# State read of both halves of the heads at once: eight transposes into two banks, 64 records into one

## The chip, the cores and the metric

One core of one Trainium2 chip runs the whole program. The metric is device time in microseconds (us); lower is better. A quoted time is the median of several executions; a profile is one execution of its own.

## What is computed

Attention between tokens and a small state, both ways, and then a feed-forward layer over all rows. Cut to what matters:

```python
B, H, S, Ns, D = 8, 8, 512, 32, 64          # x: (B,H,S,D), state: (B,H,Ns,D), fp32
a  = softmax(x @ state.T / sqrt(D));  xread = a @ state      # 512 rows per batch
a2 = softmax(state @ x.T / sqrt(D));  sread = a2 @ x         # 32 rows per batch: the state read
y  = concat([xread, sread], axis=2) as (B*544, 512)          # d_model 512
h  = y @ w_in;  g = h - tanh(h);  out = g @ w_out            # d_ff 2048
```

## The kernel before

The 4096 token rows go through the feed-forward layer as eight chunks of 512 rows, one per batch, and the 256 state rows as a ninth. A chunk is 16 steps. A step's `hidden(f)` makes one 128-row slice of h in a bank of the pool `ps_h` (two banks) by six matmuls of 512 columns (L461 to L463), then tanh on ScalarE (ACT) and subtractions on VectorE (DVE) make g. `output(f)`, two steps later, adds twelve matmuls (L508 to L510) into four output banks. These matmuls, and those of lines L922 in the second half of the run, are called the main matmuls here; their names are hps, ops, X and Y.

Chunks 0 to 3 run in this way. Chunks 4 to 7 are taken two at a time by `Pair`, whose products (L922, X and Y) take weights back from DRAM (W0m, W1m) and where DVE adds and subtracts whole pieces of g (names G, g0m, g1m). Chunk 8 is the state rows.

Beside the main matmuls stands side work. It is cut into units by `yield`, and a table gives the step at which each unit is written (`ASIDE`, keyed att1 to att7, a0, r1, m0; `SIDES` for the pairs). A scheduler then orders each engine's instructions, with `issue_after` and `high_priority` as its bounds. Each engine runs its list in order, so a matmul that waits holds all that stand behind it. Side work that matters here:

- `attention(b)`: loads xT of both halves of the heads, scores (`all_scores`, names sps, 16 short records into two banks), softmax on DVE and ACT.
- `state_read(b)` (names s, pps, p2t, rps, sr): for each half hf in turn, a softmax of s (`reduce_max` on DVE, Exp on ACT, 1/sum on DVE), a load of xn, four 128x128 transposes of s into one bank (pps), one copy to p2t on ACT, a yield, then 16 matmuls (32 records in a profile) of 32 weight columns and 64 moving columns into a second bank (rps), which are held together by `issue_after` and `high_priority`, and four scaled copies into `sr` on ACT, another yield. Batches 0 and 1 run it late, under the table's keys a0 and r1.
- `m_units` (m0 in the table): products mps and mls, copied by ACT to `st` and `sl` and stored to DRAM by 8 DMAs of the SP queue per unit (md<-st, md<-sl).

`free` is every copy out of the pool `ps_a` (two banks); each is issued after the one before. `behind_free(made)` makes a matmul wait for the last such copy, so that two banks are taken together. pps, rps, sps and mps all live in `ps_a`. The tiles of xT and xn share two buffers (tag "x"), so the loads of the next batch's xT wait until the matmuls on xn are through. All DMAs of this part are issued by SP, in order.

Of the kernel before, what the change touches and what calls it, by code (L numbers as in the profile page):

```python
# [19 lines left out]
P = 128  # L20
# [15 lines left out]
def attention_ffn(ctx: ExitStack, tc: tile.TileContext, xT, xn, bd, bh, sp, sm, sl, win, wout, xout, tout, sout):  # L36
# [10 lines left out]
    nc = tc.nc  # L47
# [6 lines left out]
    ps_a = ctx.enter_context(tc.tile_pool(name="ps_a", bufs=2, space=PSUM))  # L54
# [14 lines left out]
    ident = cpool.tile([P, P], F32, name="ident")  # L69
# [15 lines left out]
    def bank(p, name):  # L85
        return p.tile([P, 512], F32, tag=p.name, name=name)
# [105 lines left out]
    def free(out, src, **more):  # L192

        with ExitStack() as behind:
            if freed[0] is not None:
                behind.enter_context(tc.issue_after(freed[0]))
            made = nc.scalar.activation(out, src, AF.Copy, **more) if more else nc.scalar.copy(out, src)
        freed[0] = made.ins

    def behind_free(made):  # L200
        if freed[0] is not None:
            info = mybir.DependencyInfo(mybir.DependencyClass.Sync, mybir.DependencyReason.DATA)
            tc.add_manual_dep(made.ins, freed[0].name, info, reason="both banks free")
# [85 lines left out]
    def attention(b, aT):  # L289
# [76 lines left out]
        if b >= EARLY_S:  # L366
            yield from state_read(b, ss)
        else:
            late[b] = ss
# [4 lines left out]
    def late_read(b):  # L374
        yield from state_read(b, late[b])
# [3 lines left out]
            split(aTs[0][:, 0, hf], aTs[0][:, 1, hf], ats[hf])  # L379

    def state_read(b, ss):
        for hf in range(2):

            s = ss[hf]
            m2 = pool.tile([P, 1], F32, tag="m2", name=f"m2{b}{hf}")
            nc.vector.reduce_max(m2, s, axis=AX.X)
            nm = pool.tile([P, 1], F32, tag="nm", name=f"nm{b}{hf}")
            nc.vector.tensor_scalar_mul(nm, m2, -SCALE)
            rs = pool.tile([P, 1], F32, tag="rs", name=f"rs{b}{hf}")
            nc.scalar.activation(s, s, AF.Exp, bias=nm, scale=SCALE, accum_out=rs)  # L390
            ri = pool.tile([P, 1], F32, tag="ri", name=f"ri{b}{hf}")
            nc.vector.tensor_scalar_add(ri, rs, EPS)
            nc.vector.reciprocal(ri, ri)
            xr = pool.tile([P, 4, 256], F32, tag="x", name=f"xn{b}{hf}", bufs=XB)
            with tc.issue_after(loadlog[min(len(loadlog) - 1, XH)]):
                nc.sync.dma_start(xr, xn[b, hf])
            ps = bank(ps_a, f"pps{b}{hf}").rearrange("p (k n) -> p k n", n=P)
            for k in range(4):
                nc.tensor.transpose(ps[:, k], s[:, k * P : (k + 1) * P], ident)
            pt = pool.tile([P, 4, P], F32, tag="p2t", name=f"p2t{b}{hf}", bufs=PTB)  # L400
            free(pt, ps)
            yield

            ps = bank(ps_a, f"rps{b}{hf}")[:, :64]
            run = []
            for k in range(4):
                for c in range(4):
                    cs = slice(32 * c, 32 * c + 32)
                    j = TURN[c] if b < 2 else c
                    with ExitStack() as behind:  # L410
                        if run:
                            behind.enter_context(tc.issue_after(run[-1]))
                            behind.enter_context(tc.high_priority())
                        made = nc.tensor.matmul(  # L414
                            ps[cs], pt[:, k, cs], xr[:, k, 64 * j : 64 * j + 64], start=(k == 0), stop=(k == 3)
                        )
                    run.append(made.ins)
            for j in range(4):
                h = 4 * hf + (TURN[j] if b < 2 else j)
                js = slice(32 * j, 32 * j + 32)  # L420
                free(
                    sr[b // 4][32 * (b % 4) : 32 * (b % 4) + 32, 64 * h : 64 * h + 64],
                    ps[js],
                    scale=ri[js],
                )
            yield

    def turn_sread():
        srT = pool.tile([P, 2, 4, 256], F32R, tag="aT", name="srT", bufs=AB)
# [154 lines left out]
    xrs = [pool.tile([P, 2, 512], F32, tag="x", name=f"xT0{hf}", bufs=XB) for hf in range(2)]  # L584
# [12 lines left out]
    wb, mps, sps_ps, hps, ss = {}, {}, {}, {}, {}  # L597
# [99 lines left out]
    FILL = json.loads('[1, 0, 1, 2]')  # L697
    afters = [firstDVE[0], tanhs[0][1], tanhs[1][1]]
    a0 = state_read(0, ss)
    split_first()  # L700
    late1 = late_read(1)
# [3 lines left out]
    for p in range(2):  # L705
# [13 lines left out]
        a0=[1, 1, 3, 3],  # L719
# [14 lines left out]
    if "att0" in SCH:  # L734
# [4 lines left out]
        "att1": D0["att"]["1"],  # L739
        "att2": [16 + x for x in (3, 4, 5, 6, 6, 8, 8, 9, 9)],  # L740
        "m0": [17, 18, 19, 20, 22, 23, 24, 25, 26, 27, 28, 29, 30, 31, 33, 34],
        "att3": [30, 31, 31, 32, 33, 35, 36, 37, 38],
        "a0": [38, 40, 42, 44],
        "att5": [39, 40, 41, 42, 43, 45, 46, 48, 49],
        "att4": [46, 47, 48, 49, 50, 53, 55, 57, 59],
        "att6": [62, 62, 62, 63],
        "r1": [52, 54, 56, 58],
    }
    AHEAD = [54, 56, 58, 60, 62, 63]
    KEEP = [20 + x for x in range(16)]  # L750
# [222 lines left out]
    for n, duo in enumerate(duos):  # L973
        a, b = duo.a.i, duo.b.i
# [112 lines left out]
```

## Time and profile before

| what | us |
|---|---|
| median of 3 runs | 673.16 (672.67 to 675.13) |
| the profiled execution | 671.88 |
| its span, first to last instruction | 670.1 |
| TensorE matmuls busy in it | 640.1 (96%) |
| TensorE weight loads busy | 494.6 (74%) |
| VectorE busy | 485.0 (72%) |
| ScalarE busy | 391.3 (58%) |

The rows below come from views of that one execution. A timeline row gives the start and the length of one instruction or of a run of equal ones (xN), and in brackets how long the engine had been idle and whose end released it. Since matmuls overlap, a busy time says little of TensorE's pace: the distance from one start to the next does.

### The profile page before, as it was taken

The page shows a single profiled execution, that of the slowest core. Times are in us where ns is not written, and L with a number is a line of the kernel's source. Part 1 is how long each engine was busy: PE and PEld are TensorE (multiplying, and loading weights), DVE is VectorE, ACT ScalarE, POOL GpSimd, SP SyncE. Part 2 cuts the span into 40 slices and gives each one's busy share as a digit, 9 for nine tenths or more (in the row PEclk, how much of TensorE's full clock was granted, in tenths as well). Part 3 has the DMA queues.
Part 4 walks back from the last instruction along what each step waited for, and adds up shares of the span by engine and source line. Part 5 has one row for each costly group of instructions (what it writes and reads, how often), then busy time and mean ns, then how long its engine had stood idle before and what let it go on. Part 6 is the DMA issues. An engine that isn't in the chain of part 4 may idle for free.

```text
span 670.1 us, 9663 instructions
## 1 busy us (share of the span) xinstructions
PE 640.1 (96%) x3482; PEld 494.6 (74%) x3482; DVE 485.0 (72%) x769; ACT 391.3 (58%) x675; POOL 26.9 (4%) x41
## 2 busy tenths in 40 slices
PE   6778989999999999999999999999999999999997
PEld 3446666677766677787787777778888888788996
DVE  5999998639545597989735958896965689754442
ACT  3768874658655576675745667445665654543532
POOL 2000000000000000000000000000000000333300
PEclk9899998999999999999999999999999999999999
DMA  9798897466758876646722444564565535899800
GB/s 310 212 346 320 279 373 246 138 181 188 214 169 260 252 228 210 217 140 209 249 97 100 138 147 144 200 204 142 157 189 169 177 126 158 285 327 334 283 28 31
DMA packets 65199, 137.01 MB, mean 204 GB/s; under 512 B 6784, under 2 KB 28544, under 8 KB 65152
## 3 DMA queue, kind: packets, MB, share of 16 engines
q1 hardware_dynamic: 62592, 128.02, 58.8%
q0 software_dynamic: 2560, 8.39, 3.7%
q8 instruction: 27, 0.44, 0.3%
q14 instruction: 20, 0.16, 0.1%
HBM read 93.91 MB, written 42.47 MB: 204 GB/s over the span
## 4 chain that ended last, share of the span: by engine, by line
PE 55%; DVE 8%; DMA 3%; ACT 2%; SPq 1%; issue 1%; ACTq 0%; DVEq 0%
PE X L922 11%; PE hps L461 7%; PE hps L463 6%; PE hps L462 6%; PE Y1m L922 5%; PE ops L508 4%; PE ops L510 4%; PE ops L509 4%; PE Y0m L922 4%; DMA md<-st 1%; DMA mr<-md 1%; DVE G L475 1%; DVE m L101 1%; PE rps L414 1%; SPq L247 1%
## 5 line engine op out<-in xcount | busy, mean ns | idle before, releaser
L509 PE MATMUL ops<-wo,g 128*128 128x512 f32 x256 | 100.9, 398 | 5.4 <-DVE wo L101 5.4
L461 PE MATMUL hps<-aT,m 128*128 128x512 f32 x248 | 100.0, 405 | 5.0 <-DVE G L475 2.0
L508 PE MATMUL ops<-wo,g 128*128 128x512 f32 x256 | 95.8, 403 | 1.3 <-ACT wo L101 0.8
L462 PE MATMUL hps<-aT,m 128*128 128x512 f32 x248 | 97.0, 391 | 0.0
L463 PE MATMUL hps<-aT,m 128*128 128x512 f32 x248 | 96.5, 391 | 0.0
L510 PE MATMUL ops<-wo,g 128*128 128x512 f32 x256 | 93.2, 399 | 0.1
L477 DVE TENSOR_TENSOR t<-hps,t 128x512 f32<-128x512 f32 (+1 forms) x78 | 49.0, 630 | 48.3 <-ACT t L477 47.9
L475 ACT ACTIVATE t<-hps 128x512 f32<-128x512 f32 x64 | 38.2, 598 | 53.9 <-PE hps L463 53.8
L477 ACT ACTIVATE t<-hps 128x512 f32<-128x512 f32 (+1 forms) x78 | 43.0, 554 | 45.0 <-PE hps L463 42.6
L475 DVE TENSOR_TENSOR G<-hps,t 128x512 f32<-128x512 f32 x64 | 43.7, 687 | 32.3 <-ACT t L475 32.3
L461 PEld LDWEIGHTS hps<-aT,m 128*128 128x128 f32 x248 | 46.5, 188 | 24.4 <-DVE G L475 4.5
L508 PEld LDWEIGHTS ops<-wo,g 128*128 128x128 f32 x256 | 48.3, 190 | 19.4 <-ACT wo L101 2.9
L509 PEld LDWEIGHTS ops<-wo,g 128*128 128x128 f32 x256 | 48.5, 190 | 18.1 <-DVE wo L101 7.6
L101 ACT CAST g<-t 128x512 fp32r<-128x512 f32 (+1 forms) x78 | 44.9, 578 | 25.3 <-DVE t L477 24.6
L101 DVE TENSOR_TENSOR g<-t,g 128x512 fp32r<-128x512 f32 (+1 forms) x78 | 48.8, 629 | 13.1 <-ACT g L101 12.7
L510 PEld LDWEIGHTS ops<-wo,g 128*128 128x128 f32 x256 | 48.6, 191 | 11.3 <-DVE g L101 0.5
L463 PEld LDWEIGHTS hps<-aT,m 128*128 128x128 f32 x248 | 46.6, 188 | 10.4 <-DVE m L101 0.4
L462 PEld LDWEIGHTS hps<-aT,m 128*128 128x128 f32 x248 | 46.8, 189 | 8.8
L922 PE MATMUL X<-g0m,W0m 128*128 128x512 f32 x192 | 47.2, 391 | 0.4 <-DVE g0m L101 0.4
L960 POOL DMA_DIRECT2D wl<-wod x32 | 23.3, 729 | 600.1 <-DVE g1m L101 563.9
L922 PE MATMUL X<-g1m,W1m 128*128 128x512 f32 x192 | 46.0, 391 | 0.6 <-DVE g1m L101 0.6
L101 ACT CAST g1m<-G 128x1024 fp32r<-128x1024 f32 x28 | 29.2, 1054 | 28.9 <-PE Y1m L922 12.7
(257 smaller groups left out, 1131.3 us busy)
## 6 DMA issues: line engine op xcount, KB each, us to landing
mr<-md SPq DMA_DIRECT2D x24, 512.0 KB, 3.9
xT<-in_xT SPq DMA_DIRECT2D x16, 512.0 KB, 4.9
wod<-wo SPq DMA_DIRECT2D x32, 256.0 KB, 5.7
md<-st SPq DMA_DIRECT2D x64, 128.0 KB, 2.4
xn<-in_xn SPq DMA_DIRECT2D x16, 512.0 KB, 5.0
wsd<-ws SPq DMA_DIRECT2D x16, 512.0 KB, 4.8
W0m<-wsd SPq DMA_DIRECT2D x16, 512.0 KB, 4.1
W1m<-wsd SPq DMA_DIRECT2D x16, 512.0 KB, 4.5
```

The source lines that it names most:

```text
L101: return nc.scalar.copy(hi, src), (sub or nc.vector).tensor_sub(lo, src, hi)
L247: nc.sync.dma_start(dst.rearrange("h n f -> n h f"), stage[32 * j : 32 * j + 32])
L461: nc.tensor.matmul(ps, mhi[k][:, cols], ahi[:, k], start=(k == 0), stop=False)
L462: nc.tensor.matmul(ps, mhi[k][:, cols], alo[:, k], start=False, stop=False)
L463: made = nc.tensor.matmul(ps, mlo[k][:, cols], ahi[:, k], start=False, stop=(k == nk - 1))
L475: main(nc.scalar.activation(t, ps, AF.Tanh), nc.vector.tensor_sub(g, ps, t))
L477: tanhs.append((nc.scalar.activation(t, ps, AF.Tanh).ins, nc.vector.tensor_sub(t, ps, t).ins))
L508: nc.tensor.matmul(o, g[:, 0, tok], w[:, 0], start=(f == 0), stop=False)
L509: nc.tensor.matmul(o, g[:, 0, tok], w[:, 1], start=False, stop=False)
L510: return nc.tensor.matmul(o, g[:, 1, tok], w[:, 0], start=False, stop=(f == NFF - 1)).ins
L922: made = nc.tensor.matmul(out[t], w[:, e, x, cols], y[:, e], start=first and j == 0 and e == 0 and c == 0, stop=last and j == 3 and e == 1 ...
L960: nc.gpsimd.dma_start(wo[f][:, :, cols].bitcast(F32), wod[:, f % 2, half, f // 2])
```

## The change

`state_read` first does the softmax of both halves (a yield after each), then both loads of xn, then all eight transposes in a row into two banks (half 1 first; the first of them waits by `behind_free` for the last copy out of `ps_a`), both copies to p2t, a yield, and then 32 matmuls (64 records) in a row into one bank, half 0 in columns 0 to 63 and half 1 in columns 64 to 127. Eight scaled copies follow. The number of yields stays at four. The table's steps of att3, a0, att5, att4 and r1 are rewritten. No instruction is added or taken away.

```diff
@@ -379,6 +379,7 @@
             split(aTs[0][:, 0, hf], aTs[0][:, 1, hf], ats[hf])
 
     def state_read(b, ss):
+        ris, xrs, pts = [], [], []
         for hf in range(2):
 
             s = ss[hf]
@@ -391,18 +392,34 @@
             ri = pool.tile([P, 1], F32, tag="ri", name=f"ri{b}{hf}")
             nc.vector.tensor_scalar_add(ri, rs, EPS)
             nc.vector.reciprocal(ri, ri)
+            ris.append(ri)
+            yield
+        for hf in range(2):
             xr = pool.tile([P, 4, 256], F32, tag="x", name=f"xn{b}{hf}", bufs=XB)
             with tc.issue_after(loadlog[min(len(loadlog) - 1, XH)]):
                 nc.sync.dma_start(xr, xn[b, hf])
-            ps = bank(ps_a, f"pps{b}{hf}").rearrange("p (k n) -> p k n", n=P)
+            xrs.append(xr)
+        pss = [bank(ps_a, f"pps{b}{hf}").rearrange("p (k n) -> p k n", n=P) for hf in range(2)]
+        run = []
+        for hf in (1, 0):
             for k in range(4):
-                nc.tensor.transpose(ps[:, k], s[:, k * P : (k + 1) * P], ident)
+                with ExitStack() as behind:
+                    if run:
+                        behind.enter_context(tc.issue_after(run[-1]))
+                        behind.enter_context(tc.high_priority())
+                    made = nc.tensor.transpose(pss[hf][:, k], ss[hf][:, k * P : (k + 1) * P], ident)
+                if not run:
+                    behind_free(made)
+                run.append(made.ins)
+        for hf in range(2):
             pt = pool.tile([P, 4, P], F32, tag="p2t", name=f"p2t{b}{hf}", bufs=PTB)
-            free(pt, ps)
-            yield
-
-            ps = bank(ps_a, f"rps{b}{hf}")[:, :64]
-            run = []
+            free(pt, pss[hf ^ 1])
+            pts.insert(0, pt)
+        yield
+
+        ps = bank(ps_a, f"rps{b}")
+        run = []
+        for hf in range(2):
             for k in range(4):
                 for c in range(4):
                     cs = slice(32 * c, 32 * c + 32)
@@ -412,18 +429,23 @@
                             behind.enter_context(tc.issue_after(run[-1]))
                             behind.enter_context(tc.high_priority())
                         made = nc.tensor.matmul(
-                            ps[cs], pt[:, k, cs], xr[:, k, 64 * j : 64 * j + 64], start=(k == 0), stop=(k == 3)
+                            ps[cs, 64 * hf : 64 * hf + 64],
+                            pts[hf][:, k, cs],
+                            xrs[hf][:, k, 64 * j : 64 * j + 64],
+                            start=(k == 0),
+                            stop=(k == 3),
                         )
                     run.append(made.ins)
+        for hf in range(2):
             for j in range(4):
                 h = 4 * hf + (TURN[j] if b < 2 else j)
                 js = slice(32 * j, 32 * j + 32)
                 free(
                     sr[b // 4][32 * (b % 4) : 32 * (b % 4) + 32, 64 * h : 64 * h + 64],
-                    ps[js],
-                    scale=ri[js],
+                    ps[js, 64 * hf : 64 * hf + 64],
+                    scale=ris[hf][js],
                 )
-            yield
+        yield
 
     def turn_sread():
         srT = pool.tile([P, 2, 4, 256], F32R, tag="aT", name="srT", bufs=AB)
@@ -739,12 +761,12 @@
         "att1": D0["att"]["1"],
         "att2": [16 + x for x in (3, 4, 5, 6, 6, 8, 8, 9, 9)],
         "m0": [17, 18, 19, 20, 22, 23, 24, 25, 26, 27, 28, 29, 30, 31, 33, 34],
-        "att3": [30, 31, 31, 32, 33, 35, 36, 37, 38],
-        "a0": [38, 40, 42, 44],
-        "att5": [39, 40, 41, 42, 43, 45, 46, 48, 49],
-        "att4": [46, 47, 48, 49, 50, 53, 55, 57, 59],
+        "att3": [29, 30, 30, 31, 32, 33, 34, 35, 36],
+        "a0": [37, 38, 38, 39],
+        "att5": [39, 40, 40, 41, 42, 43, 44, 45, 46],
+        "att4": [46, 47, 47, 48, 49, 55, 56, 57, 59],
         "att6": [62, 62, 62, 63],
-        "r1": [52, 54, 56, 58],
+        "r1": [50, 51, 52, 53],
     }
     AHEAD = [54, 56, 58, 60, 62, 63]
     KEEP = [20 + x for x in range(16)]
```

Three places show what the order becomes. On TensorE (PE), in chunk 2, the state read of batch 3; before, with rps30 half 0's product and pps31 half 1's transposes:

```order
L509 MATMUL ops2_2_2188<-wo6_614,g2_6_2383 128x512
L510 MATMUL ops2_2_2188<-wo6_614,g2_6_2383 128x512
L508 MATMUL ops2_3_2189<-wo6_614,g2_6_2383 128x512
L509 MATMUL ops2_3_2189<-wo6_614,g2_6_2383 128x512
L414 MATMUL rps30_2386<-xn30_2350,p2t30_2357 32x64 x16
L399 MATMUL pps31_2456<-ident_72,s31_2109 128x128 x4
L510 MATMUL ops2_3_2189<-wo6_614,g2_6_2383 128x512
```

and PE in the changed kernel, at the product of that batch (its eight transposes stand 27 main matmuls ahead):

```order
L485 MATMUL hps2_9_2560<-aT2_1254,m22_2505 128x512
L483 MATMUL hps2_9_2560<-aT2_1254,m22_2505 128x512
L484 MATMUL hps2_9_2560<-aT2_1254,m22_2505 128x512
L431 MATMUL rps3_2403<-xn30_2358,p2t31_2374 32x64 x16
L431 MATMUL rps3_2403<-xn31_2360,p2t30_2372 32x64 x16
L485 MATMUL hps2_9_2560<-aT2_1254,m22_2505 128x512
L530 MATMUL ops2_0_2194<-wo7_691,g2_7_2479 128x512
```

The two halves' products are one run. On ACT, late in chunk 1, the copies of two mps pairs to st (the units m0); before:

```order
L197 ACTIVATE sr0_79<-rps21_1684,ri21_1672 32x64 x4
L197 COPY st13_1722<-mps16_1708 128x512
L197 COPY st13_1722<-mps17_1709 128x512
L101 CAST wst21_1820<-w120_1763 128x512
L197 COPY st20_1782<-mps20_1768 128x512
L197 COPY st20_1782<-mps21_1769 128x512
L101 CAST wst22_1877<-w121_1875 128x512
```

and ACT there in the changed kernel:

```order
L197 COPY st13_1721<-mps16_1707 128x512
L197 COPY st13_1721<-mps17_1708 128x512
L101 CAST wst21_1819<-w120_1762 128x512
L101 CAST ws10_1913<-wa1_1906 128x1024
L499 ACTIVATE t1_13_1813<-hps1_13_1806 128x512
L101 CAST g1_13_1816<-t1_13_1813 128x512
L197 COPY st20_1781<-mps20_1767 128x512
L197 COPY st20_1781<-mps21_1768 128x512
```

A step's tanh and cast now stand between the two pairs; on PE 18 main matmuls stand between mps16/17 and mps20/21, which were next to each other. On ACT, in the first pair of chunks, the copies of batch 6 around the tanh of chunk 5's steps 4 to 6; before:

```order
L101 CAST m52_4136<-mr52_4134 128x1024
L197 COPY p2t61_4068<-pps61_4063 128x512
L475 ACTIVATE t5_4_4089<-hps5_4_4082 128x512
L475 ACTIVATE t5_5_4114<-hps5_5_4107 128x512
L101 CAST g0m600_4281<-G4_0_3309 128x1024
L197 ACTIVATE sr1_80<-rps61_4139,ri61_4058 32x64 x4
L475 ACTIVATE t5_6_4131<-hps5_6_4124 128x512
```

and ACT there in the changed kernel:

```order
L101 CAST m52_4109<-mr52_4107 128x1024
L497 ACTIVATE t5_4_4062<-hps5_4_4055 128x512
L497 ACTIVATE t5_5_4087<-hps5_5_4080 128x512
L197 ACTIVATE sr1_80<-rps6_4112,ri60_3894 32x64 x4
L197 ACTIVATE sr1_80<-rps6_4112,ri61_3948 32x64 x4
L101 CAST g0m600_4274<-G4_0_3346 128x1024
L497 ACTIVATE t5_6_4104<-hps5_6_4097 128x512
```

Eight copies stand in a row between the tanh of steps 5 and 6, where four stood.

## Rows read from the trace of the kernel before

**Rows 1.** The page, busy time of TensorE: us, share, instructions.
```profile
PE 640.1 (96%) x3482; PEld 494.6 (74%) x3482; DVE 485.0 (72%) x769; ACT 391.3 (58%) x675; POOL 26.9 (4%) x41
```
**Rows 2.** Waits of PE, 168 to 540 us: us in total, times, longest.
```profile
PE hps L461 <- DVE G L475: 2.0, 4, 1.1
PE mps L232 <- ACT st L197: 1.2, 1, 1.2
PE hps L461 <- DVE t L477: 0.8, 1, 0.8
PE X L922 <- DVE g0m L101: 0.4, 1, 0.4
PE ops L508 <- ACT ob L522: 0.4, 1, 0.4
```
**Rows 3.** Groups by line and shape: busy us, mean ns | idle before.
```profile
L197 ACT ACTIVATE sr<-rps,ri 32x64 f32<-32x64 f32 x64 | 19.6, 306 | 8.4 <-PE rps L414 7.6
...
L414 PE MATMUL rps<-xn,p2t 128*32 128x64 f32 x512 | 10.5, 222 | 0.0
...
L399 PE MATMUL pps<-ident,s 128*128 128x128 f32 x64 | 9.7, 274 | 0.0
```
**Rows 4.** Timeline of PE, 253 to 268 us: start, us; one rps run alone.
```profile
265.94 0.39 PE L508 MATMUL ops<-wo,g 128*128 128x512 f32 x1
266.17 0.39 PE L509 MATMUL ops<-wo,g 128*128 128x512 f32 x1
266.49 0.65 PE L414 MATMUL rps<-xn,p2t 128*32 128x64 f32 x32
267.07 0.50 PE L510 MATMUL ops<-wo,g 128*128 128x512 f32 x1
267.40 0.40 PE L508 MATMUL ops<-wo,g 128*128 128x512 f32 x1
```
**Rows 5.** Timeline of PE, 281 to 283 us: four transposes alone.
```profile
281.38 0.39 PE L510 MATMUL ops<-wo,g 128*128 128x512 f32 x1
281.61 0.60 PE L399 MATMUL pps<-ident,s 128*128 128x128 f32 x4
...
282.28 0.40 PE L509 MATMUL ops<-wo,g 128*128 128x512 f32 x1
```
**Rows 6.** Timeline of PE, 527 to 530 us: six transposes of another tile.
```profile
528.16 0.82 PE L433 MATMUL tps<-ident,sr 128*128 128x128 f32 x6
...
529.05 0.40 PE L462 MATMUL hps<-aT,m 128*128 128x512 f32 x1
```
**Rows 7.** Timeline of PE, 253 to 268 us: rps with pps behind it.
```profile
259.84 0.65 PE L414 MATMUL rps<-xn,p2t 128*32 128x64 f32 x32
...
261.15 0.39 PE L508 MATMUL ops<-wo,g 128*128 128x512 f32 x1
```
**Rows 8.** Timeline of PE, 190 to 202 us: two mps pairs together.
```profile
193.62 0.96 PE L232 MATMUL mps<-wst,sms 64*128 64x512 f32 x6
195.75 0.98 PE L232 MATMUL mps<-wst,sms 64*128 64x512 f32 x6 [1.17 <-ACT st L197]
```
**Rows 9.** Timeline of ACT at the end of chunk 1.
```profile
216.97 0.58 ACT L522 COPY ob<-ops 128x512 f32<-128x512 f32 x1 [3.02 <-DMA out_x<-ob]
```
**Rows 10.** Timeline of SP's DMA issues ahead of that copy.
```profile
210.18 1.93 SPq L247 DMA_DIRECT2D md<-st  x4
212.20 2.24 SPq L251 DMA_DIRECT2D md<-sl  x4
214.54 0.84 SPq L525 DMA_DIRECT2D out_x<-ob  x2
```
**Rows 11.** Stretches: PE, PEld, DVE, ACT, POOL busy, PEclk, DMA share, GB/s.
```profile
112.00:116.00 4.00, 4.00 (x12) 3.14 (x11) 2.45 (x4) 0.62 (x1) 0.00 (x0) 0.57 0.77 262
251.00:255.00 4.00, 4.00 (x50) 3.11 (x49) 2.39 (x4) 2.06 (x3) 0.00 (x0) 1.00 0.94 337
```
**Rows 12.** Loads of xT (tile view): us from issue to landing.
```profile
DMA to landing us min/median/max: 3.4/4.9/7.8
```

## The prediction

> **What bounds the kernel now.** The first view is the page's busy times: TensorE is busy for 640.1 of 670.1 us [rows 1], so the question is what it spends on each thing and where it waits. The pace comes from the starts in a timeline: two main matmuls that follow each other start 0.23 us apart [rows 4]. The second view is the list of whom TensorE waits for from 168 us, where the first state read begins, to 540 us, behind the last [rows 2]: five rows, 2.0 + 1.2 + 0.8 + 0.4 + 0.4 = 4.8 us in all. What stands ahead of 168 us has the same order in both kernels and stays out of the sum. So in the stretch that the change touches TensorE is the bound nearly everywhere. A saved slot on it moves the end, and DVE, ACT and the DMAs count only where they make one of those waits, or a new one.
>
> **The runs on TensorE.** One product of half the heads stands alone at 266.49 us [rows 4]: from the main matmul ahead of it (266.17) to the second one behind it (267.40) are 1.23 us, of which two paces are 0.45, so it costs 0.78 us. From its first record to the next main matmul's start are 0.58 us for 32 records, 18 ns each; the other 0.20 us is the change from 128-column weights to 32-column ones and back. That part is paid once for each run, however long it is. 64 records in one run should cost 64 x 0.018 + 0.20 = 1.36 us against 2 x 0.78 = 1.56. That is 0.20 us for each of 8 batches, **1.6 us**. The section on key properties of the Trainium skill's page "TensorEngine Tiling (Array Packing)" says that a change of tiling mode, but not of the tile within a mode, drains the engine; the 0.20 us agrees with it.
>
> Four transposes cost 281.38 to 282.28 less two paces, 0.90 - 0.45 = 0.45 us [rows 5]. From the first record to the second main matmul behind are 0.67 us for these four, and 0.89 us for six of another tile [rows 6]: 0.11 us for each transpose and nothing for the run as such. Eight in a row cost what two runs of four cost, **0**. Three times before, a product had the next half's transposes right behind it; such a pair takes 1.31 us from its first record to the second main matmul behind [rows 7], 0.40 more than the product alone (0.91, [rows 4]) where transposes alone take 0.45. These 3 x 0.05 = 0.15 us are lost. Sum for the runs: 1.45 us less (bounds 1.3 and 1.6; the counts, 512 and 64 records, stay [rows 3]).
>
> **Waits that the new order takes away.** At 193.62 us two mps pairs stand next to each other, and the second waits 1.17 us for ACT to empty the two banks [rows 8]. In the new order 18 main matmuls stand between them, 18 x 0.23 = 4.1 us, in which ACT has time for two copies. With the slow restart (the first distance after a stop is 0.1 us longer) I take **1.2 us** (bounds 0 and 1.3: nothing, if the unit meets another busy bank).
>
> The end of chunk 1 is the other place. ACT's copy of an output bank waited 3.02 us for an earlier output's store [rows 9], which SP issued only at 214.54 us, behind an unbroken row of 8 stores [rows 10]. TensorE then waited 0.4 us for the bank and 0.8 us for a tanh behind that copy [rows 2]. The mps16/17 unit now runs about 30 main matmuls (7 us) earlier, and its 8 stores, some 4 us of SP's time by the two rows, leave the queue ahead of that store. I take the wait as gone, **1.3 us** with its restarts (bounds 0, if SP is as late as before, and 2.0, if the short stops around it go too).
>
> **Waits that it adds.** In the product run no instruction can slip in. Its 1.2 us are in the 1.36 us. The eight copies behind it hold ACT for 8 x 0.306 = 2.45 us in a row [rows 3], 1.22 us longer than four. Behind them on ACT stand tanh and the cast of g. In chunks 1 to 3 g is needed two steps later; from a slice's last matmul to the output that reads it are some 36 main matmuls, 8 us, and tanh, subtraction, cast and subtraction need about 3, so 2.45 us fit. In the first pair, batch 6, the two banks are wanted sooner: the scores of batch 7 come 12 main matmuls (2.7 us) after step 5's slice, and ACT must have done that step's tanh (0.6 us) and all eight copies, 3.2 us with the hand-over. I take **0.5 us** more there (bounds 0 and 1.2).
>
> Both xn are now loaded together, and both xT of the next batch wait for the one run. SP is in order, so what stands behind the first xT (for batch 7 mr53 and W0m60) waits with it. The nearest row is the landing of an xT load, 3.4 to 7.8 us, median 4.9 [rows 12]; the second is issued some 0.4 us after the first, so both are there after 5.3 us, 8.2 at worst. Between the run and the scores that need them stand 35 main matmuls (batches 5, 4), 30 (batch 6) and 36 (batch 7): 6.8 to 8.2 us. I take **0** (bounds 0 and 1.4, the worst landing against 30 matmuls).
>
> The second half's max, Exp and reciprocal run one unit earlier, at the cost they had. In chunk 2 and in the pair DVE is nearly full, and the 2.0 and 0.4 us of waits for G and g0m [rows 2] are set by its order. They can shrink or grow; I take **0** (bounds 0.7 less, 1.2 more).
>
> **The sum.** -1.45 - 1.2 - 1.3 + 0.5 = -3.45 us. The profiled execution took 671.88 us (span 670.1 and 1.8 around it), so it would take 668.4. The median of the runs is 673.16; the same difference gives 669.7 us, a ratio of 0.995.
>
> **The rivals.**
> 1. Only the runs gain. The waits on banks and stores come back elsewhere, since the number of stores and copies is the same: 673.16 - 1.45 = 671.7. For it speaks that SP is full for 20 us around 210 us [rows 10]; against it that the unit's stores move to a place ahead of that stretch. 0.22.
> 2. Slower, by ACT. The eight copies in a row hold tanh for 2.45 us, and a bank of hps or of ps_a is late by up to the extra 1.22 us [rows 3]. If that happens at all 8 batches it costs 9.8 us against the 3.95 of gains: 673.16 + 9.8 - 3.95 = 679.0. Above about three batches the gain is gone, above six the kernel is slower by 0.5%. For it speaks that ACT already waited 7.6 us for these products, with all behind it idle [rows 3]; against it the slack of 5 us in chunks 1 to 3, where six of the eight batches lie. The section on the PSUM bottleneck of the same page of the skill speaks for this rival: tiling speeds up the matmuls and not the copies out of the banks, which become the limit. No run here shows that yet. 0.11, most of it in part (674 to 676).
> 3. The clock falls. After the stops near 110 us TensorE ran for 3 us at a granted clock of 0.57, that is for the most part at its lower level [rows 11], seven distances of 0.43 us in place of 0.23, 1.4 us in all. A fall behind each of 8 runs would cost 11 us: 681. Against it: in 251 to 255 us, with a product and transposes in a row, the clock is 1.00 [rows 11], and a longer run without a pause does not look like a stop. 0.03.
> 4. More than the sum: DVE's relief in chunk 2 and in the pair takes 1.5 us more out of the waits for G and g0m: 668.2. 0.10.
>
> **How the numbers follow.** The forecast, 669.7, has 0.54: my terms hold to within 1.5 us. Rival 4 has 0.10, rival 1 0.22, rival 2 0.11, rival 3 0.03. 0.5% is 3.4 us, about what a measurement of this kernel can tell from no change: the bounds are 669.8 and 676.5. The forecast lies on the first of them, so I give it a little over two thirds of its 0.54 to faster (the bound of 2.0 at the chunk's end is open on that side) and the rest to same: 0.38 + 0.10 from rival 4 is 0.48 faster. Same is 0.16 + 0.22 + 0.05 of rival 2, 0.43. Slower is 0.06 + 0.03, 0.09. The range runs from 667.4 (rival 4 with the larger bounds) to 673.6 (rival 2 with a few batches), which leaves some 0.12 above and 0.06 below.
>
> **What would show it.** Each product run should have 64 records, with 1.17 us from the first to the next main matmul, and cost 1.36 us by the reckoning above; 1.56 would mean that the change of weights is not paid once for a run. The row of mps waiting for ACT st should be gone, and that of ops for ACT ob with the 3.02 us on ACT; if they are there again with other names, rival 1 is right. A wait of sps for ACT sr near 415 us shows the term of 0.5; waits of hps or sps for ACT in several batches show rival 2, waits of sps for xT the loads; PEclk below 0.9 after 160 us rival 3. The prediction is wrong if DVE, relieved of nothing, only waits longer for G in the pair: the sum then gives its gains back before 450 us.

## The result and the profile after

The changed kernel takes 664.19 us (median of 6 runs, 662.42 to 666.37), the kernel before 672.91 beside it (6 runs): a ratio of 0.9872, interval 0.9849 to 0.9896. Measured again among the experiments it is 0.9894 (0.9877 to 0.9912). The forecast was 669.7 with 667.4 as the lower end. The sign was right, the size was not: 3.45 us were forecast, 7 to 9 measured.

The profiled execution of after took 662.42 us (span 660.6), 9.45 less than that of before. Not all of this is the change. Ahead of 168 us TensorE's order is the same in both kernels, but before's profile has the fall of the clock at 112 us [rows 11] and the first one of after has not; a second profile of the same changed kernel has one again. The same stretch in these two (columns as in [rows 11]):

```profile
112.00:116.00 4.00, 4.00 (x20) 3.29 (x19) 2.37 (x4) 0.92 (x2) 0.00 (x0) 1.00 0.77 262
```
```profile
112.00:116.00 4.00, 2.55 (x7) 2.04 (x8) 3.83 (x7) 0.76 (x2) 0.00 (x0) 0.75 0.63 198
```

PEclk is 1.00 in the first and 0.75 in the second, so this differs from one execution to the next. To leave it out I count main matmuls on TensorE. All kernels have 2488 of them; numbers 440 and 1840 (counted from 0) stand just ahead of the first state read and behind the last, and the distance between their starts holds everything that the change touches. These are the two rows of before, then the two of after:

```profile
166.93 0.39 PE L508 MATMUL ops<-wo,g 128*128 128x512 f32 x1
538.35 0.62 PE L922 MATMUL X<-g1m,W1m 128*128 128x512 f32 x2
```
```profile
165.18 0.39 PE L530 MATMUL ops<-wo,g 128*128 128x512 f32 x1
529.10 0.62 PE L944 MATMUL X<-g1m,W1m 128*128 128x512 f32 x2
```

538.35 - 166.93 = 371.4 us before, 529.10 - 165.18 = 363.9 after: **7.5 us less**. The second profile of after has 364.1. This distance, called **the stretch** below, repeats to 0.2 us in the two profiles of after, where single times of one kernel scatter by 2 to 4 us. The kernel before has one profile, and 0.4 of its 371.4 us are a stop at 256 us that no other profile has (below), so the change itself is worth some 7.1.

What TensorE waits for in 168 to 540 us of after (us in total, times, longest), against [rows 2]:

```profile
PE hps L483 <- DVE G L497: 1.3, 2, 1.1
PE sps L324 <- ACT sr L197: 0.5, 1, 0.5
PE X L944 <- DVE g0m L101: 0.5, 1, 0.5
```

The waits for st, t and ob are gone, two of the four for G too, and the wait for sr is new. The runs, against [rows 4] and [rows 5]: one product of 64 records, and eight transposes.

```profile
262.98 0.39 PE L483 MATMUL hps<-aT,m 128*128 128x512 f32 x1
263.30 1.10 PE L431 MATMUL rps<-xn,p2t 128*32 128x64 f32 x64
264.33 0.50 PE L484 MATMUL hps<-aT,m 128*128 128x512 f32 x1
264.67 0.40 PE L485 MATMUL hps<-aT,m 128*128 128x512 f32 x1
```
```profile
257.10 0.39 PE L532 MATMUL ops<-wo,g 128*128 128x512 f32 x1
257.34 1.03 PE L410 MATMUL pps<-ident,s 128*128 128x128 f32 x8
258.13 0.48 PE L483 MATMUL hps<-aT,m 128*128 128x512 f32 x1
258.44 0.40 PE L484 MATMUL hps<-aT,m 128*128 128x512 f32 x1
```

By the prediction's own reckoning (main matmul ahead to the second one behind, less two paces) the product costs 264.67 - 262.98 - 0.45 = 1.24 us, not 1.36 (from the first record to the next main matmul 1.03, not 1.17), and the transposes 258.44 - 257.10 - 0.45 = 0.89, as forecast.

### The profile page after: what moved, and what is told of

Same layout as the page of the kernel before. It is cut to its first block, busy times and chain, and to the rows that moved or that the text cites. A ratio compares the mean times of both kernels' runs of the same rounds, so it can differ in the third digit from the quotient of the medians.

```text
span 660.6 us, 9657 instructions
## 1 busy us (share of the span) xinstructions
PE 633.5 (96%) x3482; PEld 494.4 (75%) x3482; DVE 483.8 (73%) x769; ACT 389.2 (59%) x675; POOL 27.3 (4%) x41
## 4 chain that ended last, share of the span: by engine, by line
PE 77%; DVE 14%; DMA 4%; issue 3%; ACT 2%; SPq 0%; ACTq 0%; DVEq 0%
PE X L944 12%; PE hps L483 9%; PE hps L484 8%; PE hps L485 8%; PE ops L532 8%; PE ops L531 8%; PE ops L530 8%; PE Y1m L944 5%; PE Y0m L944 4%; PE mps L232 2%; PE mls L239 2%; PE rps L431 1%; DVE m L101 1%; DMA wo3d<-in_wout 1%; DVE w L131 1%
## 5 line engine op out<-in xcount | busy, mean ns | idle before, releaser
L531 PE MATMUL ops<-wo,g 128*128 128x512 f32 x256 | 99.9, 394 | 6.0 <-DVE wo L101 6.0
L530 PE MATMUL ops<-wo,g 128*128 128x512 f32 x256 | 94.1, 396 | 0.9 <-ACT wo L101 0.8
L532 PE MATMUL ops<-wo,g 128*128 128x512 f32 x256 | 90.5, 394 | 0.0
```

Of the source, the lines that this page charges most:

```text
L530: nc.tensor.matmul(o, g[:, 0, tok], w[:, 0], start=(f == 0), stop=False)
L531: nc.tensor.matmul(o, g[:, 0, tok], w[:, 1], start=False, stop=False)
L532: return nc.tensor.matmul(o, g[:, 1, tok], w[:, 0], start=False, stop=(f == NFF - 1)).ins
```

## The experiments

Each stands beside runs of the kernel before. The last column is the stretch in the run's profile, 371.4 in the kernel before.

| kernel | median us | ratio to before (interval) | stretch |
|---|---|---|---|
| after_again | 664.99 | 0.9894 (0.9877 to 0.9912) | 364.1 |
| table_only | 671.85 | 0.9993 (0.9978 to 1.0008) | 371.5 |
| new_b2 | 668.69 | 0.9937 (0.9919 to 0.9955) | 367.6 |
| new_b67 | 671.27 | 0.9984 (0.9971 to 0.9998) | 370.3 |
| old_b2 | 668.53 | 0.9960 (0.9941 to 0.9980) | 368.5 |
| twice | 671.00 | 0.9993 (0.9975 to 1.0011) | 371.0 |
| exp_late | 663.70 | 0.9882 (0.9860 to 0.9903) | 363.8 |
| prod_early | 663.48 | 0.9875 (0.9852 to 0.9898) | 363.3 |
| store_pool | 671.19 | 0.9992 (0.9966 to 1.0018) | 371.9 |
| m0_early | 668.39 | 0.9956 (0.9938 to 0.9974) | 368.0 |
| store_act | 671.80 | 1.0009 (0.9989 to 1.0030) | 371.0 |

### Which part brings the gain

**after_again**, the changed kernel unaltered. 

> The changed kernel once more, beside the single-part kernels. Its first profile has no fall of the granted clock at 112 to 116 us (before's has one, 1.4 us), so 9.45 us between the two profiles would be about 8 us of the change. If that is so, the ratio is 0.9865 to 0.9885 and the 662.4 us of the first profile is at the low end; a profile with the fall would be near 664. The new waits at PE hps <- DVE G (1.3, 2) and PE sps <- ACT sr (0.5, 1) should be there again in 168 to 540 us, and no other row above 0.5.

The waits are there as expected, but for the row for G, which has one wait of 1.1 us in place of two. The ratio lies a little above the band, with the band's upper part in its interval; the profile has the clock's fall and took 666.55 us, more than the 664 expected for such a one.

**table_only**, the read of before with the new steps:

```diff
-        "att3": [30, 31, 31, 32, 33, 35, 36, 37, 38],
+        "att3": [29, 30, 30, 31, 32, 33, 34, 35, 36],
```

and a0, att5, att4 and r1 as in the change. 

> The read of before, one half at a time, with the table's new steps. Theory A (the gain sits in the new read: one product run in place of two, and the places where chunk 1 and the pair are relieved): PE's order is that of before up to batch 3, so the waits at 193 us (1.17) and of ACT for a store at 217 us (3.02) stay, and the time is within 1.5 us of before, ratio 0.998 to 1.002. Rival B (the gain is the table: side work of batches 3, 4, 5 and of r1 at better steps): 2 to 3.5 us less, ratio 0.995 to 0.997, though chunk 1's waits stay.

Theory A: the table alone is worth nothing.

**new_b2** and **new_b67**, the new read for some batches only, at the old table:

```diff
     def state_read(b, ss):
+        yield from (new_read if b in (2,) else old_read)(b, ss)
```

with `(6, 7)` in the second. 

> The new read for batch 2 alone, at the old table; seven batches are read as before. Everything differs from before between 168 and 215 us only. Theory A (chunk 1's three waits, 193.6, 215 to 221 and 256 us, hang on this one read: 1.2 + 2.2 + 0.4, and one run in place of two gives 0.34): 4.0 us less, ratio 0.994. As the prediction had it (1.2 + 1.3 + 0.18): 2.7 us less, 0.996. Rival (the store's row at SP is as late as before, so only the bank and the run gain): 1.5 us less, 0.998, with an ACT copy of ob waiting about 3 us near 217 us.

> The new read for batches 6 and 7 alone, the two of the first pair, at the old table. Theory A (the ledger of the pair: two runs, 2 x 0.34 = 0.7; the stops of 0.35, 0.68 and 0.16 us at 385, 402 and 409 us gone with their restarts, 1.4; the new wait of batch 7's scores for ACT's eight copies, 0.6): 1.0 to 1.7 us less, ratio 0.9975 to 0.9985. Rival (the pair's stops are set by DVE's order, which moves with chunks 2 and 3 as well): only the runs less the new wait, 0.1 us, ratio 1.000, with the stops still there. The wait of sps for sr near 409 to 415 us, 0.5 us, is expected in both.

Theory A for new_b2. One batch of eight brings half of the whole: its stretch is 3.8 us shorter, and its waits of TensorE in 168 to 540 us are these:

```profile
PE hps L533 <- DVE G L547: 2.1, 4, 1.1
PE X L994 <- DVE g0m L101: 0.5, 1, 0.5
```

All of chunk 1's rows are gone. new_b67 brings 1.1 us, at the low end of theory A; of the stops that it expected to vanish in the pair, the one at 385 us stayed. **old_b2** undoes batch 2 in the changed kernel (`b in (0, 1, 3, 4, 5, 6, 7)`). 

> The changed kernel with batch 2 alone read as before, one half at a time; the other seven batches and the table stay changed. Theory A (chunk 1's waits hang on this one read): the waits of mps for st (1.2) and of ops and hps near 215 to 221 us (1.2 and restarts) are back, and the time is 3.5 to 4.2 us above the changed kernel, ratio to before 0.994 to 0.996. Rival (the parts lean on each other: the new table or the other reads have taken the pressure off chunk 1 as well): 0.3 to 1.5 us above the changed kernel, ratio 0.990 to 0.992, the 3-us wait of ACT's copy of ob not there.

Theory A again: 4.6 us of stretch come back, 3.9 of them up to main matmul 700 (247 us in after), and with them the rows that batch 2 had taken away:

```profile
PE mps L232 <- ACT st L197: 1.2, 1, 1.2
PE hps L533 <- DVE t L549: 1.0, 1, 1.0
```

### What a run costs

**twice**, each product computed two times over in its run, with the output unchanged:

```diff
-        for hf in range(2):
+        for hf in (0, 1, 0, 1):
```

> The changed kernel, in which each product of the state read is computed twice over in the same run, half 0, half 1, half 0, half 1: 128 records where there were 64, into the same bank with the same values. It prices a record apart from what a run costs as such. Theory A (a run costs 0.34 us as such and 14 ns for each record, from 0.786 us for 32 and 1.233 for 64): 2.13 us for each run on TensorE, 8 x 0.90 = 7.2 us more than the changed kernel, ratio to before 0.999 to 1.001. Rival (18 ns for each record and 0.20 for the run, as predicted; 64 records then have another reason to be short): 2.50 us by the reckoning, 2.38 by what 64 measured, 9.2 us more, ratio 1.002 to 1.004.

Timeline of TensorE in twice, one of the eight runs:

```profile
181.50 0.39 PE L532 MATMUL ops<-wo,g 128*128 128x512 f32 x1
181.82 1.99 PE L431 MATMUL rps<-xn,p2t 128*32 128x64 f32 x128
183.74 0.50 PE L483 MATMUL hps<-aT,m 128*128 128x512 f32 x1
184.08 0.40 PE L484 MATMUL hps<-aT,m 128*128 128x512 f32 x1
```

184.08 - 181.50 - 0.45 = 2.13 us, as theory A says. 32, 64 and 128 records cost 0.79, 1.24 and 2.13 us: 0.014 us for each record and 0.34 for the run. The stretch is 7.1 us longer than after's, eight times 0.89.

### Chunk 1

Is it the new read that relieves chunk 1, or only the places that it gives the mps units? **m0_early** keeps the old read and moves one unit:

```diff
-        "m0": [17, 18, 19, 20, 22, 23, 24, 25, 26, 27, 28, 29, 30, 31, 33, 34],
+        "m0": [17, 18, 19, 20, 22, 23, 24, 23, 26, 27, 28, 29, 30, 31, 33, 34],
```

> The kernel before, its read of both halves one at a time, with one number of the table changed: the mps unit of step 25 is written at step 23. Its products then stand ahead of the second half's transposes, and 12 main matmuls, the transposes and the product of that half stand between mps16/17 and mps20/21, which were next to each other. Theory A (the read matters in chunk 1 only because its two halves push a unit against the next; any order that spreads the units does the same): the 1.17-us wait for st is gone, the 3.02-us wait of ACT for a store shrinks to under 1 us, and the time is 2.5 to 3.7 us below before, ratio 0.9945 to 0.9965. Rival (one run and one run of transposes in place of two each leave more slots between the units, which no move of one unit gives): only the 1.17 us go, 1.0 to 1.4 us, ratio 0.998, and the stops at 215 to 221 us stay or come earlier.

Theory A. TensorE has no wait for st, t or ob left, and ACT's copy of ob waits 0.38 us where [rows 9] has 3.02:

```profile
216.32 0.59 ACT L522 COPY ob<-ops 128x512 f32<-128x512 f32 x1 [0.38 <-DMA out_x<-ob]
```

One number of the table is worth 3.5 us of stretch in the kernel before, 3.1 of them in chunk 1 (new_b2: 3.8 and 3.5, with 0.34 of its run). **store_pool** and **store_act** asked whether the store's place in SP's row [rows 10] had made that copy wait; they issue chunk 1's output stores from another queue:

```diff
-            nc.sync.dma_start((xout[i] if i < B else sout)[t * P : (t + 1) * P], ob)
+            (nc.gpsimd if i == 1 else nc.sync).dma_start((xout[i] if i < B else sout)[t * P : (t + 1) * P], ob)
```

with `nc.scalar` in the second. 

> The kernel before, with the stores of chunk 1's output taken from SP's queue and given to POOL's; the state read and the table are as before. Theory A (the copies of ob on ACT and DVE near 217 us waited 3 us because the store of the earlier output stood in SP's row behind the stores of the mps units): that wait of 3.02 us is gone, and with it PE's stops for ob and t between 215 and 221 us; the wait of 1.17 us for st at 193 us stays. 1.3 to 2.2 us less than before, ratio 0.9965 to 0.998. Rival (the stores are slow to land, wherever they are issued, or ob waits for something else): the same time, 0.999 to 1.001, with an ACT wait of 2 to 3 us for out_x near 217 us.

The rival has the time. The timelines of POOL and of ACT show why: POOL issues the store at 210.40, and ACT's copy still starts only at 215.04. The three lines after them are from tile views, from issue to landing: the stores of ob in 205 to 225 us of store_pool; the same stores, from SP, in the kernel before; and the stores of st that SP issued in 208.7 to 211.2 us of store_pool, around POOL's first one.

```profile
210.40 0.70 POOL L525 DMA_DIRECT2D out_x<-ob  x1 [197.93 <-ACT ob L522]
```
```profile
215.04 0.59 ACT L522 COPY ob<-ops 128x512 f32<-128x512 f32 x1 [2.30 <-DMA out_x<-ob]
```
```profile
DMA to landing us min/median/max: 3.3/4.2/4.6
```
```profile
DMA to landing us min/median/max: 2.1/2.4/2.8
```
```profile
DMA to landing us min/median/max: 3.9/4.1/4.3
```

Most of what the early issue won, the slower landing took back: ACT's wait is 0.7 us shorter, and TensorE has a new one of 1.0 us for sl. POOL's queue need not be the reason. SP's stores of st, half as large (128 KB), took 3.9 to 4.3 us when they were issued at that moment, so a store is slow to land there from either queue. In the key constraints of the Trainium skill's page "Trainium Kernel Development and Optimization" it is said that DMAs of the SP, ACT and POOL queues run on the same engines, so that issuing from several saves issue time only; the time agrees, 0.9992.

> The kernel before, with the stores of chunk 1's output issued from ACT's queue, right behind the copies there, in place of SP's row of mps stores. From POOL's queue the store was issued 4.1 us earlier (210.40 against 214.54) but took 4.6 us to land, where SP's take 2.1 to 2.8, so the wait for it only fell from 3.02 to 2.30 us. Theory A (SP's row made the store late; POOL's path gave it back): issued at about 211.4 and landed at 213.8 to 214.5, the ACT copy of ob waits 0 to 0.7 us, PE's stops between 215 and 221 us are gone, 1.3 to 2.2 us less than before, ratio 0.9965 to 0.998. Rival (the stores land late because the DMA engines are full there, whoever issues): landing at 215 to 216 us, a wait of 1.5 to 2.3 us left, 0 to 0.6 us less, ratio 0.999 to 1.000.

Neither theory. ACT issued the store at 213.04, not at 211.4; the copy of ob no longer waited, but the copy to st did, for other stores (timelines of SP and of ACT):

```profile
208.71 1.83 SPq L247 DMA_DIRECT2D md<-st  x4
```
```profile
213.04 0.86 ACTq L525 DMA_DIRECT2D out_x<-ob  x2
214.02 1.07 ACT L197 COPY st<-mps 128x512 f32<-128x512 f32 x2 [4.05 <-DMA md<-sl]
```

What held ACT's issue can be read from the semaphores in the trace. The DMAs of SP and ACT take eight semaphores in turn, and an issue waits until the DMA that had its semaphore before has landed: here the store of st that SP issued at 208.71, which landed at 212.97. In the kernel before, the store of [rows 10] was issued at 214.54, and its semaphore came free at 214.46, with the landing of the store of st issued at 210.18. So with landings as they are, a shorter row of SP's issues would not have let it out sooner; no run changed the semaphores. No single store is to blame. Three mps units with 24 stores stand too close, and whichever buffer is needed next is late. What helps, by new_b2 and m0_early, is to spread the units.

### The first pair

**exp_late** writes the second half's max and Exp of batch 6 one unit later, at the step of the transposes:

```diff
-            "att6": [0, 9, 14, 20, 26],
+            "att6": [0, 9, 20, 20, 26],
```

> The changed kernel, in which the second half's max and Exp of batch 6 stand one unit later in the pair, with the transposes (near where they stood before); the run of 64 stays. Theory A (the stops of PE for G at 385 and 402 us went because this max left its old place on DVE): a stop of 0.6 to 0.7 us for G near 400 us is back and the time is 0.7 to 1.1 us above the changed kernel, ratio to before 0.990. Rival (they went because chunks 2 and 3 are shorter and DVE comes into the pair with less behind it): no such stop, and the same time as the changed kernel, 0.989, within 0.4 us.

In the trace transposes and product stand 30 main matmuls later than in after, at the places that the second half's had in the kernel before. Theory A falls: no stop of that size near 400 us is back, and the time is the same. (Its wait for sr is gone too; short stops for G, 0.28 us at 393 and 0.17 more at 420, take that gain.) The trace of before has another cause for its stop at 402.68 us. ACT's four copies of half 0 stood between the casts of two pieces of g0m; DVE waited 1.12 us for the second cast, and G's subtraction stands behind that. ACT, DVE and TensorE of before:

```profile
397.37 1.05 ACT L101 CAST g0m<-G 128x1024 fp32r<-128x1024 f32 x1 [0.76 <-DVE G L475]
398.44 1.26 ACT L197 ACTIVATE sr<-rps,ri 32x64 f32<-32x64 f32 x4
399.72 1.05 ACT L101 CAST g0m<-G 128x1024 fp32r<-128x1024 f32 x1
```
```profile
400.80 1.23 DVE L101 TENSOR_TENSOR g0m<-G,g0m 128x1024 fp32r<-128x1024 f32 x1 [1.12 <-ACT g0m L101]
401.94 0.68 DVE L475 TENSOR_TENSOR G<-hps,t 128x512 f32<-128x512 f32 x1
```
```profile
402.68 0.50 PE L461 MATMUL hps<-aT,m 128*128 128x512 f32 x1 [0.52 <-DVE G L475]
```

In the changed kernel no copy of sr stands there. That this removed the stop is read from the order, with new_b67 for it (there the stop is gone too); no run took these four copies away alone.

**prod_early** writes batch 6's product one step earlier:

```diff
-            "att6": [0, 9, 14, 20, 26],
+            "att6": [0, 9, 14, 20, 24],
```

> The changed kernel, with the product of batch 6 written one step earlier in the table. TensorE runs it at the same place, but ACT's eight copies then stand ahead of the tanh of step 5, where ACT was idle for 2 us, and the scores of batch 7 stand 6 main matmuls earlier. Theory A (the 0.54-us wait of sps is ACT's queue, not the copies' own time): the wait of sps for sr is gone and nothing takes its place, 0.5 to 0.7 us less than the changed kernel, ratio to before 0.988. Rival (the copies hold tanh of step 5 and hps waits for it, or G is later by them): the same time as the changed kernel within 0.3 us, with a new wait of hps for t or G of some 0.5 us between 404 and 412 us.

In after, ACT's eight copies stand behind a tanh for which ACT sat idle 2.05 us, and TensorE waits for them (timelines of ACT and TensorE):

```profile
405.97 0.60 ACT L497 ACTIVATE t<-hps 128x512 f32<-128x512 f32 x1 [2.05 <-PE hps L485]
406.60 2.54 ACT L197 ACTIVATE sr<-rps,ri 32x64 f32<-32x64 f32 x8
```
```profile
409.19 1.09 PE L324 MATMUL sps<-xT,bdr 64*32 64x512 f32 x16 [0.54 <-ACT sr L197]
```

In prod_early the copies come first and nothing waits:

```profile
405.07 0.60 ACT L497 ACTIVATE t<-hps 128x512 f32<-128x512 f32 x1
405.70 2.53 ACT L197 ACTIVATE sr<-rps,ri 32x64 f32<-32x64 f32 x8
408.26 0.60 ACT L497 ACTIVATE t<-hps 128x512 f32<-128x512 f32 x1
```
```profile
408.97 1.09 PE L324 MATMUL sps<-xT,bdr 64*32 64x512 f32 x16
```

Theory A: 0.6 us off the stretch, at 363.3 the shortest of all. This one number makes a kernel whose stretch beats both; the medians (663.48, ratio 0.9875) agree but can't tell 0.6 us from after.

## Why the prediction was wrong

The working is the prediction's; here is each term against the stretch.

| term | forecast | measured |
|---|---|---|
| product runs, transposes, adjacency | -1.45 | -2.6 |
| the distances right behind each run | not seen | -0.35 |
| chunk 1: bank wait and chunk end | -2.5 | -3.2 |
| eight copies ahead of batch 7's scores | +0.5 | +0.6 |
| DVE order, stops in the pair | 0 | -1.4 |
| the stop at 256 us | not seen | -0.4 |
| sum | -3.45 | -7.35 |

The stretch fell by 7.5. The steps that failed are three terms of the sum: the cost of a run as such was put at 0.20 us and is 0.34, the end of chunk 1 at 1.3 us and it gave some 2.0, and DVE's order at 0, where stops worth 1.4 us went.

- **The runs.** I took the 0.58 us from the first record to the next main matmul and divided by 32: 18 ns a record, 0.20 for the run. But this span holds part of the run's fixed cost. From two lengths it is 14 ns and 0.34, which is 2 x 0.79 - 1.24 = 0.34 us a batch, 2.7 in all, less 0.15 for the adjacency, as forecast. For the transposes I had two lengths (four and six), and that price held at eight. The mechanism, a cost paid once a run, was right. That a change of tiling mode drains the engine, by the section on key properties of the Trainium skill's page "TensorEngine Tiling (Array Packing)", fits it. The 0.34 us are for the change there and back with the run's start and end; no run takes the drain apart from these. A further 0.35 us lies in the distances from the second to the seventh behind each run, some 15 to 20 ns in all after every one: 0.59 us at before's 29 places and 0.23 at after's 16. Its cause is not shown.
- **Chunk 1.** The place and the mechanism were right, the bank wait as forecast (1.2). The chunk's end was worth about 2 us, the bound that I had called open, not 1.3. The reason given, SP's row ahead of one store, is only part of it: store_pool and store_act moved the store and won nothing, m0_early moved a unit and won nearly all (3.1).
- **The wait that was added.** Forecast at 0.5 us behind batch 6, measured 0.54, and none in chunks 1 to 3: the slack of 5 us held, and rival 2 (slower by ACT) with it fell. The section on the PSUM bottleneck of the Trainium skill's page "TensorEngine Tiling (Array Packing)", which spoke for that rival, says that the copies may become the bottleneck. Here TensorE waited for them in one batch of eight, and prod_early took that wait away by the order of ACT's queue.
- **DVE's order.** I took 0 with up to 0.7 less. The stops for G at 385 and 402 us went (0.35 and 0.68 us by the distance of starts, with two restarts of 0.11 us), and a slow distance at 409 us (0.16), as rival 4 had it, though by ACT's queue in the second and not by a relief of DVE. The stop at 256 us (0.29 and a restart) is gone too, but no other profile has it, not even that of new_b67, where the order of TensorE, ACT and DVE is that of before until 393 us; it belongs to the one execution. What sets the first stop of the pair, 0.28 us in after, 0.87 in old_b2 and two stops in before, I did not settle, so the gain at 385 us has no cause shown.
- **The loads of xT** made no wait, and the **clock** is 1.00 behind 168 us, as forecast. table_only shows that the steps bring nothing by themselves.
- **The base.** The first three runs of before had a median of 673.16; the later medians lie at 671 to 672. This shifts the forecast's absolute number by 1 to 2 us and not the ratio.

The range was too narrow. The chunk's end reached its bound (2.0). The runs (2.6 against a bound of 1.6) and the pair (1.4 against 0.7) went beyond theirs, the runs because the fixed cost of a run was given as if it had been measured.

## What to carry to other kernels

Price an operation that comes in runs from two run lengths, never from one divided by its count: the fixed part hides in the quotient, and merging runs saves just that part. When a side job changes shape, look at where its neighbours land: here the largest term came from one job no longer pushed against the next, and one number of the order table gets nearly all of that term without the change. Copies that wait in an engine's queue behind an instruction with nothing to do yet cost the whole wait; write them a step earlier.

## What the runs showed of the hardware

- Runs of 128x32-tile products of 64 columns cost 0.34 us as such and 0.014 us for each record, at 32, 64 and 128 records (0.79, 1.24, 2.13).
- How long a store takes to land went with the moment of its issue. Near 210 us of store_pool, stores of 256 KB from POOL took 4.6 us and stores of 128 KB from SP 3.9 to 4.3; in the kernel before, SP's stores of 256 KB in 205 to 225 us took 2.1 to 2.8, and its stores of 128 KB issued at 210.2 to 211.1 us 4.0 to 4.3.
- The clock's fall near 112 us comes and goes between executions of one kernel, with no change in TensorE's order there. In both profiles of after TensorE stops for 1.5 us (to 111.30 and to 113.45 us) and goes on with the same matmuls; in the first the granted clock stays at its higher level (2.4 GHz, PEclk 1.00 in 112 to 116 us), in the second it falls to the lower one (1.2 GHz) for a part of that stretch (PEclk 0.75). Seven of the 13 profiles have the fall.
